# One wait per turn in place of many: two one-element reads of the last exponential in an attention kernel, and a tanh moved between two exponentials

## The chip, the cores and the metric

The kernel runs on one core of a Trainium2 chip. A core has five engines with a queue of instructions each: TensorE (matrix products; the profile's PE, its weight loads PEld), VectorE (DVE), ScalarE (ACT), GpSimd (POOL) and SyncE (SP, which here only starts DMA transfers). An engine takes its instructions in order. Between engines, and where one instruction must see what an earlier one of the same engine has written, order is kept by semaphores that an instruction waits on. The metric is the device time of one execution in microseconds (us).

## The reference

For a sequence of 2048 rows of width 512, with 32 heads of 16 and a hidden width of 1792:

```python
xn = layernorm(x)
q, k, v = split(xn @ wqkv)                        # 32 heads of width 16
s  = softmax(q @ k.T * 16**-0.5) @ v @ wo         # attention
h  = relu(xn @ w1 + b1) ** 2                      # dense layer, squared relu
g  = silu(h @ w2 + b2)
out = x + s * g
```

## The kernel before

The first part of the kernel normalizes x and forms the keys, queries and values. The main part is a loop of 128 **turns**. A turn handles four steps; a step is a block of 128 keys against 512 queries for four heads, in two pairs of heads. For each pair the scores come from two matmuls of 64 rows each, which lie in the two halves of TensorE's array and run at the same time (`score`, line 282). ScalarE takes their exponential into a tile `ptile` in SBUF (`exps`, line 286). At the end of the turn `values` (line 561) multiplies the four steps' exponentials with the values and adds up in PSUM, in 32 matmuls of a quarter of the array each.

PSUM has two score tiles S that take turns, one bank called `single` (its tile is named lin), one bank pair called `spare`, and the accumulator `acc`. In a turn the scores come in this order: the two pairs of step 1 and the two of step 2 go through S; the two pairs of step 3 are **set aside**: each half-pair goes to `single`, VectorE copies it to SBUF (`aside`, line 305, four copies a turn), and ScalarE later takes the exponential in place (`exps(i + 3, p, ptile[...])`); then come the two pairs of the next turn's first step, through S. So the last exponential of a turn is that of the next turn's step 0, second pair. A score tile is used again when its exponential has been taken. The second score of a turn, `scores(i + 1, 1)`, uses the tile of that last exponential.

The matmuls of the dense layer and of the last projection fill in between. A `Block` is a sum of such matmuls in one bank of `spare`; `lin`, `lin_part` and `swap` (lines 330 and 350) issue them half an array at a time, a schedule written out by hand in the turn loop. Per chunk of 512 rows the list `fill` has 28 entries, one for each turn: `make` starts a pair of blocks, `end` tells whether one finishes, a third flag whether a piece of the weights is split in two at the turn's end (`split_piece`, a cast on VectorE and a subtraction on GpSimd). When a pair is complete its `evict` runs on VectorE: bias, relu, square and a cast for the first layer (lines 413, 414, 100), one addition into `y` for the second (line 429).

Other work has due times: `at(time, fn)` puts it in a table, and `happen(n)` and `happen(n + 0.5)` issue what is due at the start of turn n and near its end. Among these are row sums (lines 583 to 595), loads, and the gate of the dense layer: `gate_start` (line 606, a tanh on ScalarE) and half a turn later `gate_end` (line 612, on VectorE, then a DMA). There are eight gates. After every fourth turn (n % 4 == 3) `finish` evicts the accumulator to `ou`, on VectorE, except in 12 turns where `turn_ends_first` sends that copy to ScalarE.

The loop runs under a manual schedule: each engine's queue has the order in which the code issues. The waits are worked out from the tiles that an instruction reads and writes. A tile `ptile` was last written by an exponential of the turn before, so an exponential that writes it again waits for ScalarE's own semaphore beside that of the scores, and the first of two set-aside copies into it waits for ScalarE beside TensorE. Where an instruction has two waits, the first is an instruction of its own ahead of it (EVENT_SEMAPHORE in the trace).

Of the kernel before, what the change touches and what calls it, by code (L numbers as in the profile page):

```python
# [24 lines left out]
FT = mybir.dt.float32  # L25
# [3 lines left out]
OP = mybir.AluOpType  # L29
# [44 lines left out]
def fast_path(tc, sb, ps, env):  # L74
# [7 lines left out]
    dve, act, pool, sp = nc.vector, nc.scalar, nc.gpsimd, nc.sync  # L82
# [3 lines left out]
    def t(shape, dt, tag):  # L86

        cnt[0] += 1
        p = ps if tag in ("S", "lin", "acc") else sb
        if tag in BUFS:  # L90
            turn[tag] = turn.get(tag, -1) + 1
            n = turn[tag] % BUFS[tag]
            tag = f"{tag}{places[n] if tag == 'S' else n}"
        return p.tile(shape, dt, tag=tag, name=f"{tag}_{cnt[0]}")
# [181 lines left out]
    ptile = {}  # L276

    def score(i, p, hp, dst):
        qd, qc, kb = steps[i]
        k, q = ka[qd, kb // 8], qa[qd, qc]  # L280
        r = slice(64 * hp, 64 * hp + 64)
        mm(dst, k[r, p, 128 * (kb % 8):128 * (kb % 8) + 128], q[r, p], start=True, stop=True)  # L282

    def exps(i, p, src):
        if src is not None:
            act.activation(ptile[i, p], src, AF.Exp, scale=SCALE)  # L286

    def place(i, p):
        ptile[i, p] = t([128, 2, 512], FT, f"P{2 * ((i - 1) % 4) + p}")

    def scores(i, p):

        if i < len(steps):
            sc = t([128, 2, 512], FT, "S")
            place(i, p)
            for hp in range(2):
                score(i, p, hp, sc[:, hp])
            return sc

    def aside(i, p, hp):  # L300

        if hp == 0:
            place(i, p)
        score(i, p, hp, single)
        dve.tensor_copy(ptile[i, p][:, hp], single)  # L305
# [51 lines left out]
    def lin(*halves):  # L357
        if pair[0]:
            for half in halves:
                j = half ^ swapped[0]  # L360
                pair[0][j].issue(half, lin_banks[j])

    def lin_part(half, part):
        if pair[0]:
            j = half ^ swapped[0]
            pair[0][j].issue_part(half, lin_banks[j], part)

    def swap():
        if pair[0]:
            while any([pair[0][half ^ swapped[0]].issue(half, lin_banks[half ^ swapped[0]]) for half in range(2)]):  # L370
                pass
            swapped[0] ^= 1
            if not swapped[0]:
                pair[0][0].evict()
                pair[0] = None
# [21 lines left out]
    def split_piece(eng=None):  # L397
        if at_piece[1] == len(pieces):
            return
        j, layer, m = pieces[at_piece[1]]  # L400
        at_piece[1] += 1
        raw, q = raws.pop(0), PAIRS[m][1]
        wf[layer, m] = [t([128, 4, 256] if layer == 1 else [128, 2, 512], FR, f"wf{layer}{p}{q}") for p in "hl"]
        split(*wf[layer, m], raw, eng or dve, pool)
        load_piece()
# [15 lines left out]
    def second(c, g, i):  # L421
        ms = [m for m in range(len(PAIRS)) if PAIRS[m][0] == g]
        h, w = [hid[m] for m in ms], [wf[2, m] for m in ms]

        def evict():
            if g == 0:
                y[c, i] = t([128, 2, 512], FT, f"y{i}")
            old = b2b.unsqueeze(1).broadcast_to([128, 2, 512]) if g == 0 else y[c, i]
            dve.tensor_tensor(y[c, i], spare, old, op=OP.add)
            if g == 3:  # L430
                complete.add((c, i))

        return [Block(lambda p, k, j=j: h[k // 2][p][:, k % 2, 128 * j:128 * j + 128],
                      lambda p, k: w[k // 2][p][:, k % 2], range(2 * len(ms)), evict)
                for j in (2 * i, 2 * i + 1)]
# [7 lines left out]
    fill = []  # L443
    for c in ORDER:
        for m, (g, _) in enumerate(PAIRS):
            fill += [(lambda m=m: first(m), False), (None, True)]
            if m in (1, 2, 4, 6):
                for i in range(2):
                    make = lambda c=c, g=g if m > 1 else 0, i=i: second(c, g, i)
                    fill += [(make, True)] if m == 1 else [(make, False), (None, True)]  # L450
    per = len(fill) // NC
    fill = [(*a, n % per in (0, 2, 4, 5, 6, 8, 10, 12, 14, 16, 18, 20, 22, 24)) for n, a in enumerate(fill)]
# [96 lines left out]
    def at(time, fn, *a):  # L549

        events.setdefault(int(2 * time), []).append((fn, a))
# [3 lines left out]
    def values(i):  # L555
        qd, qc, kb = steps[i]
        if kb == 0:
            acc[0] = t([128, 512], FT, "acc")
        for j in (1, 2, 3, 0) if i % 2 else (0, 1, 2, 3):
            o = (4 * qd + j) * 17  # L560
            mm(acc[0][32 * j:32 * j + 32], vt[:, kb, o:o + 32], ptile[i, j // 2][:, j % 2],  # L561
               start=kb == 0, stop=kb == NK - 1)

    def finish(i):

        qd, qc, kb = steps[i]
        if kb < NK - 1:
            return
        if i == len(steps) - 1:
            return  # L570
        ou = t([128, 512], FT, "ou")
        cast(act if turn_ends_first[0] else dve, ou, acc[0])
        sp.dma_start(zdram[qd][qc], ou[16::32])
        for j in range(4):
            sp.dma_start(udram[qd // 2][qc][0, qd % 2, :, j], ou[32 * j:32 * j + 16])
        n = i // 4
        events.setdefault(2 * n + 2, []).insert(0, (load_sums, (qd, qc)))
        at(n + 2, rowsums, qd, qc)
# [24 lines left out]
    def gate_start(c, i):  # L603
        assert (c, i) in complete
        e = t([128, 2, 512], FT, "T")
        act.activation(e, y[c, i], AF.Tanh, scale=0.5)
        gated[c, i] = e
# [98 lines left out]
        wlast.append(a)  # L706


    TURNS, LAST = len(steps) // 4, 16 * (NQ - 1)
    for n in range(4 * NQ - 1):  # L710
        at(4 * n + 0.5, load_qa, (n + 1) // 4, (n + 1) % 4)
# [4 lines left out]
        at(8.5 + 2 * kb + 2 * (kb > 9), maxvalue, kb)  # L716
    for j, c in enumerate(ORDER):
        for i in range(2):
            at(per * (j + 1) + 2 * i - 2, gate_start, c, i)
            at(per * (j + 1) + 2 * i - 1.5, gate_end, c, i)  # L720
        if j < 3:
            at(per * (j + 1) - 3.5, load_x_parts, ORDER[j + 1])
# [25 lines left out]
    fill = [(*a, 0) if len(a) == 2 else a for a in fill]  # L748
# [4 lines left out]
    def happen(time):  # L753
        for fn, a in events.pop(int(2 * time), ()):
            fn(*a)


    n = turn["S"]
# [4 lines left out]
    single = t([128, 512], FT, "lin")  # L763
    xs[0] = xT[3]

    def rest(i, dst):

        group(dst, lambda p: onorm[2, 3][p][:, cut[i]], lambda p: wos[0][p][:, 3])

    def end_rest(i, src):  # L770

        o = t([128, 512], FT, f"wf2{'hl'[i // 2]}{i % 2}")
        dve.scalar_tensor_tensor(o, src, 0.5, gsb[2, i // 2][:, i % 2], op0=OP.mult, op1=OP.mult)
        pool.dma_start(out[1024 + 128 * i:1152 + 128 * i], o, accum_op=OP.add)

    turn_ends_first = [False]
    for n in range(TURNS):
        i = 4 * n
        happen(n)
        make, end, split_now = fill[n]  # L780
        if make:
            pair[0] = make()
        exps(i + 1, 0, scores(i + 1, 0))
        aside(i + 3, 0, 0)
        lin(1)
        exps(i + 1, 1, scores(i + 1, 1))
        for _ in range(3):
            lin(0, 1)
        lin(0)
        if make and end:  # L790
            lin(1)
            lin(0)
            aside(i + 3, 0, 1)
        else:

            lin_part(1, 0)
            aside(i + 3, 0, 1)
            lin(0)
        exps(i + 2, 0, scores(i + 2, 0))
        if make and end:  # L800
            for j in range(2):
                pair[0][j].issue_whole(lin_banks[j])
            swap()
        else:
            lin_part(1, 1)
            lin(0, 1)
            lin(0, 1)
        exps(i + 2, 1, scores(i + 2, 1))
        aside(i + 3, 1, 0)
        lin(1)  # L810
        exps(i + 3, 0, ptile[i + 3, 0])
        lin(0, 1)
        lin(0, 1)
        last = [scores(i + 4, 0)]
        lin(0, 1)
        lin(0, 1)
        lin(0)
        aside(i + 3, 1, 1)
        exps(i + 3, 1, ptile[i + 3, 1])
        last.append(scores(i + 4, 1))  # L820
        for p in range(2):
            exps(i + 4, p, last[p])
        if n == TURNS - 1:
            two = t([128, 2, 512], FT, "S")
            rest(0, two[:, 0])
        turn_ends_first[0] = n < LAST and end and fill[n][0] is None and fill[n - 1][2] and n % per in (7, 15, 23)
        swap()
        if n == LAST - 1:
            gsb.update({(2, i): y[2, i] for i in range(2)})
        if n == TURNS - 1:  # L830
            end_rest(0, two[:, 0])
        happen(n + 0.5)
        if split_now:
            split_piece()
        for j in range(4):
            values(i + j)
        finish(i + 3)
# [169 lines left out]
```

## Time and profile before

| | us |
|---|---|
| median of 3 runs | 1262.85 (1262.16 to 1263.13) |
| profiled execution | 1262.52 |
| its span, first to last instruction | 1260.7 |
| TensorE matmul busy | 1247.7 |
| ScalarE busy | 1034.2 |
| VectorE busy | 677.8 |
| GpSimd busy | 259.0 |

The granted clock of TensorE is 0.998 of full speed over the whole span. The 128 turns run from 149.56 to the last values at about 1242. Most turns are 8.5 us long. A row of a timeline has the start in us from the span's start, the length, the engine, the line of the code, the operation, output and input tiles, the shapes and a count; in brackets stands how long the engine was idle before and what ended it. Matmuls are pipelined and overlap, so that the length of one is more than the time between two; the ends are modelled. A row of the waits has who waited for whom, the sum, how often, and the longest. Rows of groups have the busy time and, after the comma, the mean length of one in ns.

### The profile page before, as it was taken

To read this page: it belongs to the slowest core of one execution; us is meant where nothing else is said; L and a number is where in the kernel's file an instruction comes from. 1 tells how busy PE (TensorE), PEld (TensorE's weight loads), DVE (VectorE), ACT (ScalarE), POOL (GpSimd) and SP (SyncE) were. 2 spreads that over 40 slices of the span, in tenths; PEclk is the share of its full clock that TensorE was granted. 3 is DMA by queue.
4 is the path that set the end of the run, shared out by engine and by line. 5 is a ranking of instruction groups with operands and counts; after the bars stand their busy time and mean duration, and the time that the engine had idled before them with its cause. 6 is when DMAs were issued, how large, how long until landed. Compare 5 with 4: busy or idle time off the path is not lost.

```text
span 1260.7 us, 24997 instructions
## 1 busy us (share of the span) xinstructions
PE 1247.7 (99%) x10029; PEld 721.5 (57%) x10029; DVE 677.8 (54%) x1064; ACT 1034.2 (82%) x1123; POOL 259.0 (21%) x150
## 2 busy tenths in 40 slices
PE   9999999999999999999999999999999999999997
PEld 7888755555555555555555555555555555555553
DVE  5542255555555654545465455555554545566655
ACT  4222588989899898999988989899889989998883
POOL 5000122122211221312023221220331212322112
PEclk9999999999999999999999999999999999999999
DMA  7565613231233232131423222333222122463444
GB/s 267 209 234 190 218 49 105 60 94 52 85 127 110 60 97 72 42 92 46 154 75 110 59 78 60 93 126 106 59 62 90 46 90 59 144 218 125 145 131 119
DMA packets 84940, 137.32 MB, mean 109 GB/s; under 512 B 26058, under 2 KB 40408, under 8 KB 83284
## 3 DMA queue, kind: packets, MB, share of 16 engines
q1 hardware_dynamic: 81668, 126.25, 30.9%
q0 software_dynamic: 2720, 8.65, 2.4%
q8 instruction: 79, 1.29, 0.4%
q10 hardware_dynamic: 432, 0.79, 0.2%
q14 instruction: 41, 0.34, 0.1%
HBM read 94.24 MB, written 41.41 MB: 108 GB/s over the span
## 4 chain that ended last, share of the span: by engine, by line
PE 97%; DVE 1%; POOL 1%; issue 0%; DMA 0%; ACT 0%; DVEq 0%; ACTq 0%
PE acc L561 36%; PE spare L330 25%; PE S L282 16%; PE S L111 9%; PE lin L282 8%; PE spare L350 1%; PE S L204 1%; PE spare L339 0%; POOL hl L104 0%; DMA P<-in_A_x_dram 0%; PE acc L111 0%; DVE P L305 0%; DVE st L166 0%; POOL wf2l L104 0%; PE spare L687 0%
## 5 line engine op out<-in xcount | busy, mean ns | idle before, releaser
L286 ACT ACTIVATE P<-S 128x1024 f32<-128x1024 f32 x768 | 732.5, 1020 | 67.6 <-PE S L282 64.5
L305 DVE COPY P<-lin 128x512 f32<-128x512 f32 x512 | 353.8, 691 | 457.5 <-PE lin L282 412.7
L561 PE MATMUL acc<-P,vt 128*32 128x512 f32 x4096 | 466.0, 595 | 0.0
L282 PE MATMUL S<-QA,KA 64*128 64x512 f32 x1536 | 335.1, 417 | 0.1
L286 ACT ACTIVATE P<-P 128x1024 f32<-128x1024 f32 x256 | 271.3, 1060 | 34.4 <-DVE P L305 34.3
L561 PEld LDWEIGHTS acc<-P,vt 128*32 128x32 f32 x4096 | 120.0, 109 | 266.4 <-issue 266.4
L282 PEld LDWEIGHTS S<-QA,KA 64*128 64x128 f32 x1536 | 147.6, 184 | 160.6 <-ACT P L286 121.6
L282 PE MATMUL lin<-QA,KA 64*128 64x512 f32 x512 | 213.7, 417 | 0.7 <-DVE P L305 0.5
L104 POOL TENSOR_TENSOR wf1l<-wr,wf1h 128x1024 fp32r<-128x1024 f32 x28 | 66.8, 2384 | 400.8 <-DVE wf1h L100 137.9
L104 POOL TENSOR_TENSOR hl<-T,hh 128x1024 fp32r<-128x1024 f32 x28 | 67.7, 2417 | 240.3 <-DVE hh L100 129.6
L330 PE MATMUL spare<-xl,wf1h 64*128 64x512 f32 x440 | 109.6, 392 | 0.0
L282 PEld LDWEIGHTS lin<-QA,KA 64*128 64x128 f32 x512 | 94.1, 184 | 26.6 <-DVE P L305 4.0
L104 POOL TENSOR_TENSOR wf2l<-wr,wf2h 128x1024 fp32r<-128x1024 f32 x28 | 66.7, 2383 | 204.2 <-PE acc L561 138.0
L330 PE MATMUL spare<-wf2l,hh 64*128 64x512 f32 x400 | 97.4, 391 | 0.0
L330 PE MATMUL spare<-xh,wf1l 64*128 64x512 f32 x504 | 96.0, 391 | 0.0
L330 PE MATMUL spare<-xh,wf1h 64*128 64x512 f32 x504 | 95.6, 390 | 0.0
L330 PE MATMUL spare<-wf2h,hh 64*128 64x512 f32 x448 | 85.7, 390 | 0.0
L330 PE MATMUL spare<-wf2h,hl 64*128 64x512 f32 x416 | 80.8, 391 | 0.0
L330 PEld LDWEIGHTS spare<-xh,wf1h 64*128 64x128 f32 x504 | 59.9, 184 | 9.5
L98 ACT CAST P<-S 128x512 fp32r<-128x512 f32 x30 | 17.6, 587 | 57.6 <-PE S L111 55.8
L330 PEld LDWEIGHTS spare<-xh,wf1l 64*128 64x128 f32 x504 | 60.4, 185 | 7.6
L330 PEld LDWEIGHTS spare<-xl,wf1h 64*128 64x128 f32 x440 | 63.0, 184 | 1.5
(210 smaller groups left out, 1108.0 us busy)
## 6 DMA issues: line engine op xcount, KB each, us to landing
wr<-in_B_w_dram SPq DMA_DIRECT2D x56, 512.0 KB
KA<-kd SPq DMA_DIRECT2D x64, 256.0 KB
QA<-qd SPq DMA_DIRECT2D x128, 128.0 KB
kd<-P SPq DMA_DIRECT2D x15, 512.0 KB
qd<-P SPq DMA_DIRECT2D x15, 512.0 KB
u<-ud SPq DMA_DIRECT2D x15, 512.0 KB
P<-in_A_x_dram SPq DMA_DIRECT2D x8, 512.0 KB
xd<-KA SPq DMA_DIRECT2D x4, 1024.0 KB
```

What stands on the lines that cost most here:

```text
L98: act.copy(dst, src)
L104: leng.tensor_tensor(lo, src, hi.bitcast(FT), op=OP.subtract)
L111: mm(dst, lhs(a, k), rhs(b, k), start=n == 0, stop=n == len(todo) - 1)
L204: nc.tensor.transpose(pt[:, k, 128 * j:128 * j + 128], xnorm[c, i][:, j, 128 * k:128 * k + 128], ident)
L282: mm(dst, k[r, p, 128 * (kb % 8):128 * (kb % 8) + 128], q[r, p], start=True, stop=True)
L286: act.activation(ptile[i, p], src, AF.Exp, scale=SCALE)
L305: dve.tensor_copy(ptile[i, p][:, hp], single)
L330: mm(bank, self.lhs(a, k)[r], self.rhs(b, k)[r], start=n == 0 and self.at[other] == 0, stop=n == len(self.todo[half]) - 1 and self.at[othe ...
L350: mm(bank[:, c], self.lhs(a, k)[r], self.rhs(b, k)[r, c], start=False, stop=False)
L561: mm(acc[0][32 * j:32 * j + 32], vt[:, kb, o:o + 32], ptile[i, j // 2][:, j % 2], start=kb == 0, stop=kb == NK - 1)
```

## The change

A helper `see` is called in each turn but the first, after the turn's first score matmuls and ahead of its first exponential. On ScalarE it copies the last element of the tile that the last exponential of the turn before wrote. On VectorE it takes the maximum of that element and one element of the score tile that this exponential read. Each of the two waits for that last exponential; instructions behind it on the same engine then don't wait for ScalarE's semaphore, where they did for an earlier exponential. A further copy on VectorE of one element of `single` stands after the turn's last set-aside copy. The conditions in `alone` leave out some turns: both engines in the eight turns with a tanh, ScalarE where it evicts the accumulator at the turn's end, VectorE where n % 4 == 3 and ScalarE does not evict.

Since VectorE now reads the score tile of the last exponential, the second score of a turn, which uses that tile again, waits for VectorE's maximum where there is one, in place of the exponential. The first set-aside score of a turn waits for the added copy of `single`.

The tanh of a gate is issued in the same turn as before, not at its start ahead of the first exponential but between the two set-aside exponentials.

```diff
+    tanh_in = {}
...
-            at(per * (j + 1) + 2 * i - 2, gate_start, c, i)
+            tanh_in[per * (j + 1) + 2 * i - 2] = c, i
...
+    seen = t([1, 16], FT, "seen")
+
+    def see(i, other, act_waits, dve_waits):
+
+        last = ptile[i, 1][:1, 1, 511:]
+        if act_waits:
+            act.copy(seen[:, :1], last)
+        if dve_waits:
+            dve.tensor_tensor(seen[:, 8:9], last, other[:1, 0, :1], op=OP.max)
+
     for n in range(TURNS):
         i = 4 * n
         happen(n)
         make, end, split_now = fill[n]
+        turn_ends_first[0] = n < LAST and end and not make and fill[n - 1][2] and n % per in (7, 15, 23)
+
+        alone = [n not in tanh_in and not turn_ends_first[0],
+                 n not in tanh_in and (n % 4 < 3 or turn_ends_first[0])]
         if make:
             pair[0] = make()
-        exps(i + 1, 0, scores(i + 1, 0))
+        pair0 = scores(i + 1, 0)
+        if n:
+            see(i, last[1], *alone)
+        exps(i + 1, 0, pair0)
         aside(i + 3, 0, 0)
...
         exps(i + 3, 0, ptile[i + 3, 0])
+        if n in tanh_in:
+            gate_start(*tanh_in[n])
         lin(0, 1)
...
         aside(i + 3, 1, 1)
+        if alone[1]:
+            dve.tensor_copy(seen[:, 8:9], single[:1, :1])
         exps(i + 3, 1, ptile[i + 3, 1])
...
-        turn_ends_first[0] = n < LAST and end and fill[n][0] is None and fill[n - 1][2] and n % per in (7, 15, 23)
         swap()
```

In the changed kernel the copy on ScalarE is line 784, the maximum on VectorE line 786 and the copy of `single` line 840; the lines named above keep their numbers up to 707.

## The prediction

> **What bounds the kernel now.** I read the page first, for the share of each engine and the chain that ended last, then the waits, then the timeline of single turns, engine by engine.
>
> ```profile
> PE 1247.7 (99%) x10029; PEld 721.5 (57%) x10029; DVE 677.8 (54%) x1064; ACT 1034.2 (82%) x1123; POOL 259.0 (21%) x150
> ...
> PE 97%; DVE 1%; POOL 1%; issue 0%; DMA 0%; ACT 0%; DVEq 0%; ACTq 0%
> ```
>
> TensorE carries 97% of the chain. ScalarE is busy 82% of the span and has room. So nothing on ScalarE or VectorE counts until it makes TensorE late, and TensorE's queue is in order: one weight load that waits holds everything behind it. The waits (us in total, times, longest) say where that can be:
>
> ```profile
> PEld S L282 <- ACT P L286: 121.6, 198, 0.8
> ACT P L286 <- PE S L282: 64.5, 107, 0.9
> ```
>
> ScalarE waits for the first score of a turn 107 times at 0.6 us each. The 121.6 us are mostly not lost: the load is fetched ahead while matmuls still run. To see what is lost I take one plain turn, turn 50 (starts 576.21). Columns: start, length, engine, line, operation. Weight loads:
>
> ```profile
> 576.55 0.19 PEld L282 LDWEIGHTS S<-QA,KA 64*128 64x128 f32 x2
> ...
> 579.07 0.18 PEld L282 LDWEIGHTS lin<-QA,KA 64*128 64x128 f32 x1
> ```
>
> Its matmuls:
>
> ```profile
> 576.55 0.39 PE L282 MATMUL lin<-QA,KA 64*128 64x512 f32 x1
> ...
> 576.79 0.39 PE L282 MATMUL S<-QA,KA 64*128 64x512 f32 x2
> 577.02 1.08 PE L330 MATMUL spare<-xh,wf1h 64*128 64x512 f32 x7
> ...
> 577.83 0.46 PE L282 MATMUL lin<-QA,KA 64*128 64x512 f32 x1
> ...
> 579.17 0.63 PE L330 MATMUL spare<-xl,wf1h 64*128 64x512 f32 x2
> ...
> 579.88 0.40 PE L282 MATMUL S<-QA,KA 64*128 64x512 f32 x2
> ```
>
> Its copies on VectorE and its exponentials on ScalarE:
>
> ```profile
> 575.85 0.69 DVE L100 CAST hh<-T 128x1024 fp32r<-128x1024 f32 x1
> 577.05 0.69 DVE L305 COPY P<-lin 128x512 f32<-128x512 f32 x1 [0.51 <-PE lin L282]
> 578.33 0.69 DVE L305 COPY P<-lin 128x512 f32<-128x512 f32 x1 [0.59 <-PE lin L282]
> ```
>
> ```profile
> 575.20 1.02 ACT L286 ACTIVATE P<-S 128x1024 f32<-128x1024 f32 x1
> 576.82 3.79 ACT L286 ACTIVATE P<-S 128x1024 f32<-128x1024 f32 x4 [0.60 <-PE S L282]
> 580.49 1.06 ACT L286 ACTIVATE P<-P 128x1024 f32<-128x1024 f32 x1
> 581.83 1.06 ACT L286 ACTIVATE P<-P 128x1024 f32<-128x1024 f32 x1 [0.28 <-DVE P L305]
> ```
>
> The two halves of the array work side by side. In the row of seven, each half has four starts, so a slot is (1.08 - 0.39) / 3 = 0.23 us. From the score at 576.79 to the score at 579.88 the code issues 26 half-array matmuls (the two half-column ones counted as one), 13 slots: 2.99 us, but 3.09 passed. So TensorE stalls about 0.09 us a turn. The last place is the load at 579.07: the copy of 578.33 ended at 579.02, the load starts 0.05 later and its neighbour's matmul 0.10 after that. Turn lengths, by the windows (busy time per engine):
>
> ```profile
> 252.56:261.06 8.50, 8.50 (x77) 4.67 (x74) 5.38 (x10) 7.62 (x8) 1.61 (x1) 1.00 0.29 81
> 576.21:584.70 8.49, 8.49 (x77) 4.66 (x73) 3.70 (x6) 7.61 (x9) 4.70 (x2) 1.00 0.00 0
> 610.15:618.85 8.70, 8.70 (x78) 4.58 (x74) 3.89 (x5) 8.44 (x10) 0.00 (x0) 1.00 0.24 94
> 1140.01:1148.77 8.76, 8.76 (x74) 4.66 (x71) 5.60 (x11) 7.70 (x8) 2.96 (x3) 1.00 0.49 156
> ```
>
> An unstalled plain turn would be 8.49 - 0.09 = 8.40.
>
> **The change, part by part: what is saved.** The first copy of a turn waits for two semaphores (line 305 against TensorE and ScalarE), the second for one. The first starts 577.05 - (576.55 + 0.39) = 0.11 after its matmul, the second 578.33 - (577.83 + 0.46) = 0.04. A second wait costs 0.07 us when the engine stands ready. Where `see` waits once, the turn's first copy and first exponential start 0.07 earlier, and the loads that stall follow: I take 0.07 of the 0.09 (bounds 0 and 0.09). A rule of the Trainium skill speaks against the gain: VectorE: DVE Perf Modes, Rules for kernel authors, says to minimize the number of operations, not of semaphores. The 0.11 and 0.04 disagree with it; it is a rival below.
>
> **What is added.** One element each: 107 copies on ScalarE (L784), 99 maxima (L786) and 100 copies (L840) on VectorE, counted over the 128 turns from the conditions in `alone`. No DMA is added or moved, and SP's and POOL's queues keep their order. Nearest rows for a small operation:
>
> ```profile
> L518 ACT ACTIVATE warm<-eps 128x1 f32<-128x1 f32 x1 | 0.2, 203 | 0.0
> ...
> L856 DVE COPY zc<-lin 128x16 f32<-128x16 f32 x1 | 0.2, 175 | 0.1
> ```
>
> ScalarE's copy waits for the last exponential to finish (576.22) and lasts some 0.20: done by 576.47, inside the idle 0.60 before 576.82. It costs nothing there; its cover is gone if it lasts over 0.5, and then every 0.1 more is a 0.1 later exponential. VectorE's maximum also reads the bank of the last score, so the **second score of the turn now waits for VectorE** in place of ScalarE, in all 99 turns. That is the main cost. In TensorE's queue stand behind this load all other matmuls of the turn. The maximum waits for the last exponential, and for everything ahead of it in VectorE's own queue; I give it 0.17 (bounds 0, if only its start counts, and 0.20, the ScalarE row). With VectorE free: 576.22 + 0.04 + 0.17 + 0.05 = 576.48, before the load of 576.55. Such a load could be 0.13 later still without loss (0.23 of a slot less the 0.10 from load to matmul). So a maximum that ends later than 0.42 into the turn stalls TensorE by the excess. VectorE is late at the start of many turns; turn 12, and the evictions of the accumulator by engine:
>
> ```profile
> 249.49 1.21 DVE L429 TENSOR_TENSOR y<-spare,y 128x1024 f32<-128x1024 f32 x1
> 252.70 0.69 DVE L100 COPY ou<-acc 128x512 f32<-128x512 f32 x1 [1.99 <-PE acc L561]
> 253.40 0.69 DVE L305 COPY P<-lin 128x512 f32<-128x512 f32 x1
> ```
>
> ```profile
> L100 DVE COPY ou<-acc 128x512 f32<-128x512 f32 x19 | 13.1, 687 | 22.9 <-PE acc L561 22.9
> ...
> L98 ACT COPY ou<-acc 128x512 f32<-128x512 f32 x12 | 7.0, 588 | 1.8 <-PE acc L561 0.6
> ```
>
> In turn 12 (starts 252.56) VectorE evicts the accumulator from 252.70 to 253.39, when TensorE has finished it, and the maximum is queued behind. An operation can start about 0.08 before the end of the one ahead (turn 116 below: the copy at 1141.14, the eviction's end at 1141.22). So the maximum runs from 0.75 into the turn, and the score's matmul starts at 0.75 + 0.17 + 0.05 + 0.10 = 1.07 to 1.09, not at 0.58. TensorE loses 0.51; with the old 0.09 gone the turn grows by 0.42. Of the 19 evictions on VectorE 15 stand ahead of a turn with a maximum: eight are like turn 12, **+3.4 us**; four come behind a cast, three in the tail:
>
> ```profile
> 184.27 0.68 DVE L100 COPY ou<-acc 128x512 f32<-128x512 f32 x1
> ...
> 1140.55 0.67 DVE L100 COPY ou<-acc 128x512 f32<-128x512 f32 x1
> 1141.14 0.67 DVE L305 COPY P<-lin 128x512 f32<-128x512 f32 x1
> ```
>
> Turn 4 starts 183.97 and its eviction ends 0.98 in: stall 0.65, less 0.09, four times 0.55: **+2.2**. Turn 116 starts 1140.01 and its eviction ends 1.21 in: stall 0.88, against 0.36 now (8.76 - 8.40, since its first copy starts late, at 1141.14), three times 0.51: **+1.5**.
>
> The other turns. The 12 that follow an eviction on ScalarE: its copy ends late, and ScalarE's one-element copy now stands between it and the first exponential.
>
> ```profile
> 218.71 0.59 ACT L98 COPY ou<-acc 128x512 f32<-128x512 f32 x1 [0.15 <-PE acc L561]
> 219.19 1.03 ACT L286 ACTIVATE P<-S 128x1024 f32<-128x1024 f32 x1
> ```
>
> Turn 8 starts 218.57, its first exponential 0.62 in. At 0.72 to 0.82 the turn is 0.09 to 0.19 longer, by the tanh turn below (0.85 gives 8.70): eleven times 0.14, **+1.5**; the twelfth, turn 108, also has a late cast, +0.6. Next, even turns behind a cast:
>
> ```profile
> 269.26 0.69 DVE L100 CAST hh<-T 128x1024 fp32r<-128x1024 f32 x1
> ```
>
> ```profile
> 1157.29 0.62 DVE L100 CAST wf1h<-T 128x512 fp32r<-128x512 f32 x1
> ```
>
> In eight (turn 50: cast done 576.54, 0.33 in) the copy of L840 in the turn before pushes the cast by 0.1: stall 0.08, which the saved 0.09 pays. In five (turn 14 starts 269.55, cast done 0.40 in) the stall is 0.16: +0.4. Three in the tail (turn 118 starts 1157.23, cast done 0.68 in): +0.4, +0.4, +0.1. In 40 turns VectorE is early: 0.07 saved each, **-2.8**. Twelve have VectorE's second wait gone and not ScalarE's: -0.03 each, -0.4. Sixteen have no maximum: their copies keep both waits, nothing.
>
> **Tanh.** It moves from ahead of the first exponential to between the set-aside ones.
>
> ```profile
> 610.05 1.06 ACT L606 ACTIVATE T<-y 128x1024 f32<-128x1024 f32 x1
> 611.00 1.02 ACT L286 ACTIVATE P<-S 128x1024 f32<-128x1024 f32 x1
> ```
>
> ```profile
> 251.59 1.04 PE L561 MATMUL acc<-P,vt 128*32 128x512 f32 x8
> ```
>
> Now it delays the first exponential to 0.85 in, and the turn is 8.70. In its new place it fills the gap of 0.28 before 581.83 and pushes the last exponential 0.6 past the next turn's start. That turn starts its exponentials at 0.85 to 0.9 (the one-element copy waits for 0.61 + 0.04 and lasts 0.2), and its second score waits as long. Eight pairs: 8.70 + 8.49 = 17.19 before, 8.49 + 8.80 after, **+0.8**. The last eight value matmuls need that set-aside exponential; they start 0.97 before the next turn (251.59 against 252.56), so at 583.73 in turn 50, and the exponential would end at 581.83 + 0.6 + 1.06 = 583.49: no stall.
>
> **Sum.** 3.4 + 2.2 + 1.5 + 1.5 + 0.6 + 0.4 + 0.9 + 0.8 - 2.8 - 0.4 = +8.1 us. The profiled execution took 1262.52 around a span of 1260.7, 0.33 below the median of 1262.85: 1262.5 + 8.1 = 1270.6.
>
> **Rivals.**
> - *Faster.* The second score is not held, because the maximum is through before 0.42 into the turn everywhere. Then the 71 turns counted above with a maximum and no eviction on ScalarE each gain 0.07: -5.0 - 0.4 + 1.5 + 0.8 = -3.1, 1259.4. It decides where that maximum ends before 0.42. For it: VectorE is busy only 54%. Against: the eviction of turn 12 ends 0.83 in and cannot end sooner, it waits for TensorE.
> - *No change.* Second scores stall half as much (the maximum counts only with its start, part is caught up): of some 12 us of stall 6 go, +2, 1264.5.
> - *The saved waits are worth nothing.* That would keep only the losses, 8.1 + 2.8 + 0.4 = +11.3: 1273.8. Against: 0.11 and 0.04 after the matmul, above. By the Trainium skill's rule above this is the outcome.
> - *ScalarE's copy is not covered.* It lasts over 0.5, since it waits for its own engine's exponential; each 0.1 beyond is 0.1 in some 95 turns, so 0.2 beyond gives 1270.6 + 19 = 1290. Against: 0.20 in the row.
>
> **How the numbers follow.** My sum 0.53, worthless waits 0.13, uncovered copy 0.09, no change 0.12, faster 0.13. A measurement of this kernel tells about 0.2%, 2.5 us, from no change. Slower is 0.53 + 0.13 + 0.09 = 0.75. The range, 1259 to 1278, takes in half of the faster case, the middle, the worthless waits and stalls up to 1.6 times mine; it leaves out the uncovered copy. The forecast's own range is 1265.5 to 1276.
>
> **What would show it.** Turn 12's second pair of weight loads (L282) waits for VectorE's maximum and starts about 1.0 into the turn, not 0.34; that turn is 8.9 long. Plain turns with VectorE early are 8.42. The first copies start 0.04 after their matmul. ScalarE's copy ends before 0.5 into a plain turn. In the waits a new row stands, weight loads of S held by VectorE, 8 to 12 us lost. I am wrong if turn 12 stays at 8.5, or if plain turns gain more than 0.09.

## The result, and the profile after

The changed kernel takes 1267.24 us (median of 7 runs, 1266.61 to 1267.74), the kernel before 1262.46 beside it (7 runs, 1262.16 to 1263.19). The ratio is 1.0036, 95% interval 1.0025 to 1.0048: **slower by 0.36%, 4.8 us**. The profiled execution has a span of 1265.4 where before had 1260.7.

The page after, busy time by engine and the chain that ended last:

```profile
PE 1246.9 (99%) x10029; PEld 715.3 (57%) x10029; DVE 693.3 (55%) x1263; ACT 1056.0 (83%) x1230; POOL 258.9 (20%) x150
...
PE 91%; DVE 4%; issue 2%; ACT 1%; POOL 1%; DMA 0%; DVEq 0%; ACTq 0%
```

The busy time of TensorE has not grown; its share of the chain fell from 97% to 91%, and VectorE's rose from 1% to 4%. The waits (us in total, times, longest) say where VectorE came in:

```profile
PEld S L282 <- ACT P L286: 123.3, 218, 0.8
...
ACT P L286 <- PE S L282: 54.4, 131, 0.7
...
PEld S L282 <- DVE seen L786: 20.3, 46, 1.1
```

The last row is new: 46 weight loads of scores are held by the maximum of line 786. It counts the whole wait of a load, also the part that TensorE, still busy with matmuls, does not feel; how much of it is lost, e1 below shows. The three added instructions, by the groups of the page (busy, mean ns of one):

```profile
L784 ACT COPY seen<-P 1x1 f32<-1x1 f32 x107 | 20.3, 190 | 3.0
...
L786 DVE TENSOR_TENSOR seen<-P,S 1x1 f32<-1x1 f32 x99 | 13.7, 138 | 79.9 <-ACT P L286 79.9
L840 DVE COPY seen<-lin 1x1 f32<-1x1 f32 x100 | 13.6, 136 | 0.0
```

Now single turns, by the windows (start and end of the turn, then its length). They are, in this order, turn 4 (behind a cast and an eviction on VectorE), 8 (behind an eviction on ScalarE), 9 (plain), 12 (behind an eviction on VectorE), 54 (with a tanh), 55 and 57 (each after a tanh, 57 with a maximum) and 116 (tail):

```profile
184.10:193.51 9.41, 9.06 (x74) 4.39 (x71) 6.21 (x14) 8.10 (x10) 3.44 (x2) 1.00 0.25 71
219.32:227.87 8.55, 8.55 (x77) 4.57 (x74) 5.11 (x13) 8.15 (x11) 3.96 (x2) 1.00 0.28 79
227.87:236.29 8.42, 8.42 (x77) 4.60 (x73) 4.09 (x8) 7.82 (x10) 0.83 (x1) 1.00 0.30 80
253.20:262.09 8.89, 8.69 (x77) 4.55 (x73) 5.43 (x13) 7.91 (x10) 1.56 (x1) 1.00 0.29 77
612.20:620.69 8.49, 8.49 (x78) 4.78 (x74) 3.99 (x5) 7.89 (x9) 0.00 (x0) 1.00 0.14 55
620.69:629.26 8.57, 8.57 (x77) 4.60 (x74) 3.90 (x5) 8.29 (x10) 0.00 (x0) 1.00 0.16 60
637.75:646.51 8.76, 8.69 (x77) 4.57 (x74) 6.20 (x11) 8.40 (x11) 2.19 (x1) 1.00 0.46 135
1143.24:1152.51 9.27, 8.67 (x76) 4.58 (x72) 5.75 (x14) 7.97 (x10) 2.96 (x3) 1.00 0.58 174
```

Turn 12 went from 8.50 to 8.89 and turn 116 from 8.76 to 9.27; the plain turn lies at 8.42. Turn 4 was 8.82 before. Why turn 12 is longer: its weight loads after, and the rows before that answer to the last two,

```profile
253.20 0.19 PEld L282 LDWEIGHTS S<-QA,KA 64*128 64x128 f32 x2 [0.84 <-ACT P L286]
...
254.14 0.19 PEld L282 LDWEIGHTS S<-QA,KA 64*128 64x128 f32 x2 [0.64 <-DVE seen L786]
254.25 0.42 PEld L330 LDWEIGHTS spare<-xh,wf1h 64*128 64x128 f32 x4
```

```profile
252.90 0.19 PEld L282 LDWEIGHTS S<-QA,KA 64*128 64x128 f32 x2
253.13 0.65 PEld L330 LDWEIGHTS spare<-xh,wf1h 64*128 64x128 f32 x6
```

and VectorE's rows after:

```profile
253.35 0.69 DVE L100 COPY ou<-acc 128x512 f32<-128x512 f32 x1 [2.01 <-PE acc L561]
253.96 0.13 DVE L786 TENSOR_TENSOR seen<-P,S 1x1 f32<-1x1 f32 x1
```

The eviction holds VectorE until 254.04, the one-element maximum runs from 253.96, 0.76 into the turn, and the load of the second score waits for its end: 0.94 into the turn in place of 0.34. That load used to be fetched 0.13 ahead of need, so what follows it is late by less than 0.60: it starts at 1.05 (254.25) in place of 0.57 (253.13), 0.47 to 0.48 later. Further on 0.09 of that is caught up, and the turn ends 0.39 longer.

All 128 turns, after less before, in the classes of the prediction (a turn's length runs from the first score load to that of the next turn; mean of the class in us, then its sum):

| turns | each | sum | predicted sum |
|---|---|---|---|
| 8 like turn 12 | +0.41 | +3.27 | +3.4 |
| 4 behind a cast too (4, 32, 60, 88) | +0.57 | +2.28 | +2.2 |
| 3 tail evictions (116, 120, 124) | +0.49 | +1.48 | +1.5 |
| 11 behind an eviction on ScalarE | +0.05 | +0.58 | +1.5 |
| turn 108 | +0.57 | +0.57 | +0.6 |
| 13 even turns behind a cast | -0.03 | -0.39 | +0.4 |
| 3 tail casts (118, 122, 126) | +0.23 | +0.69 | +0.9 |
| 8 tanh turns and the 8 behind them | -0.20, +0.15 | -0.37 | +0.8 |
| 40 early turns | -0.07 | -2.89 | -2.8 |
| 12 with VectorE's wait alone gone | -0.01 | -0.15 | -0.4 |
| 16 without a maximum | -0.01 | -0.22 | 0 |
| start of the turns, turn 0 | | +0.15 | 0 |
| sum | | +5.0 | +8.1 |

### The profile page after: what moved, and what is told of

Its sections match the earlier page's. It is cut to its first block, busy times and chain, and to the rows that moved or that the text cites. A ratio compares the mean times of both kernels' runs of the same rounds, so it can differ in the third digit from the quotient of the medians.

```text
span 1265.4 us, 24423 instructions
## 1 busy us (share of the span) xinstructions
PE 1246.9 (99%) x10029; PEld 715.3 (57%) x10029; DVE 693.3 (55%) x1263; ACT 1056.0 (83%) x1230; POOL 258.9 (20%) x150
## 4 chain that ended last, share of the span: by engine, by line
PE 91%; DVE 4%; issue 2%; ACT 1%; POOL 1%; DMA 0%; DVEq 0%; ACTq 0%
PE acc L561 32%; PE spare L330 25%; PE S L282 16%; PE S L111 9%; PE lin L282 6%; ACT P L286 1%; PE spare L350 1%; DVE T L413 1%; DVE P L305 1%; PE S L204 1%; DVE T L414 0%; DVE T L677 0%; PE spare L339 0%; POOL hl L104 0%; DVE ou L100 0%
## 5 line engine op out<-in xcount | busy, mean ns | idle before, releaser
L282 PE MATMUL S<-QA,KA 64*128 64x512 f32 x1536 | 340.0, 418 | 5.5 <-DVE seen L786 5.1
L282 PEld LDWEIGHTS S<-QA,KA 64*128 64x128 f32 x1536 | 152.7, 183 | 181.7 <-ACT P L286 123.3
L282 PE MATMUL lin<-QA,KA 64*128 64x512 f32 x512 | 206.1, 402 | 0.7 <-DVE P L305 0.5
L330 PE MATMUL spare<-xl,wf1h 64*128 64x512 f32 x440 | 105.5, 391 | 0.0
L330 PEld LDWEIGHTS spare<-xl,wf1h 64*128 64x128 f32 x440 | 60.0, 184 | 1.3
```

Of the source, the lines that this page charges most:

```text
L330: mm(bank, self.lhs(a, k)[r], self.rhs(b, k)[r], start=n == 0 and self.at[other] == 0, stop=n == len(self.todo[half]) - 1 and self.at[othe ...
```

## The experiments

The theory was that the maximum's read of the score bank costs the time, since TensorE then waits for VectorE, late in some turns, and that the saved waits gain 0.07 in each early turn. The main rival was that the added instructions cost by themselves, or the move of the tanh.

**e1: VectorE no longer reads the score bank.** It still waits for the last exponential, by copying the element that this wrote.

```diff
-            dve.tensor_tensor(seen[:, 8:9], last, other[:1, 0, :1], op=OP.max)
+            dve.tensor_copy(seen[:, 8:9], last)
```

> The changed kernel, but VectorE's one element is copied from the last exponential's tile alone and the score tile is not read, so the second score waits for ScalarE again; every saved wait stays saved. Theory 'held score' (the second score waits for VectorE's queue): turn 12 falls from 8.89 to about 8.47, turn 4 from 9.41 to about 8.87, turn 116 from 9.27 to about 8.83, the 40 early turns stay at 8.42, the turns after a tanh at about 8.57: 1257.5 us, 5 below the kernel before. Rival 'worthless waits and extra operations' (the cost lies in the 306 added operations themselves): turn 12 stays near 8.9 and the time near 1267.

Measured: 1257.31 us (1256.72 to 1258.29), ratio to the kernel before 0.9959 (0.9945 to 0.9973). Turn 12 of this kernel, which starts at 252.38, VectorE's rows and then the load of its second score:

```profile
252.53 0.69 DVE L100 COPY ou<-acc 128x512 f32<-128x512 f32 x1 [1.99 <-PE acc L561]
253.14 0.13 DVE L786 COPY seen<-P 1x1 f32<-1x1 f32 x1
```

```profile
252.73 0.19 PEld L282 LDWEIGHTS S<-QA,KA 64*128 64x128 f32 x2
```

The small instruction stands at the same place (0.76 into the turn), just as late; but nobody waits for it, and the second load is back at 0.35. Turns 4 and 12 by the windows:

```profile
183.78:192.66 8.88, 8.88 (x74) 4.61 (x70) 6.26 (x14) 8.02 (x10) 3.46 (x2) 1.00 0.30 78
252.38:260.82 8.44, 8.44 (x77) 4.65 (x73) 5.42 (x13) 7.81 (x10) 1.55 (x1) 1.00 0.30 80
```

They are 8.88 and 8.44 where the change has 9.41 and 8.89. The instruction is a copy here and a maximum there, but it lasts 0.13 in both; what differs is the operand in the score bank. That operand costs 1267.24 - 1257.31 = 9.9 us (the prediction had 8 to 12 us lost in this wait), and it alone turns a gain into a loss. By class, e1 less the change: the 8 like turn 12 -3.7, the four -2.2, the three -1.3, the tail casts -0.9, behind a tanh -0.8, casts -0.7, turn 108 -0.5.

**e2: no small instructions on VectorE in the 15 turns behind an eviction there**, all else as in the change.

```diff
...
+        if n and n % 4 == 0 and not evicted_by_act:
+            alone[1] = False
+        evicted_by_act = turn_ends_first[0]
```

> The changed kernel, but without VectorE's maximum (and the copy of single) in the turns that follow an eviction on VectorE (15 turns: 4, 12, 20, 32, ... 124); the rest as changed. Theory 'held score': these 15 turns carry 3.3 + 2.3 + 1.5 = 7.0 us, so they return to 8.49, 8.82 and 8.7 and the time to about 1260.2. Rival 'spread cost' (the loss lies in all turns with a maximum): 15 of 99 turns give back about 1 us, 1266.

Measured: 1261.10 us (1259.79 to 1261.82), ratio 0.9990 (0.9981 to 0.9999). Turns 4 and 12:

```profile
183.90:192.70 8.80, 8.80 (x74) 4.57 (x70) 6.10 (x12) 7.91 (x10) 3.48 (x2) 1.00 0.30 78
252.39:260.88 8.49, 8.49 (x77) 4.74 (x73) 5.40 (x11) 7.82 (x10) 1.60 (x1) 1.00 0.30 80
```

They are as long as before the change (8.82 and 8.50). Those 15 turns, 3.27 + 2.28 + 1.48 = 7.0 us by the table, carried the loss; 6.1 us of it came back in the median. (Two other turns of the profiled execution, 39 and 115, are 0.3 longer; the last section has them.)

**e3: the kernel before with only the tanh moved.**

```diff
...
-            at(per * (j + 1) + 2 * i - 2, gate_start, c, i)
+            tanh_in[per * (j + 1) + 2 * i - 2] = c, i
...
         exps(i + 3, 0, ptile[i + 3, 0])
+        if n in tanh_in:
+            gate_start(*tanh_in[n])
```

> The kernel before with the tanh moved alone, no one-element operations. By my prediction's step for tanh (+0.8 us in the changed kernel, with the one-element operations in the turn behind): here the turn of the tanh falls from 8.69 to 8.49 and the next grows by about 0.1 (second score waits for the exponential that ends 0.6 in): -1.6 + 0.8 = -0.8, 1261.7 us. Rival: the late exponential delays the values too, each pair costs 0.2: 1264.

Measured: 1261.74 us (1261.04 to 1262.54), ratio 0.9995 (0.9986 to 1.0004), which is no difference that this can tell. Turns 54, 55 and 57:

```profile
609.73:618.22 8.49, 8.49 (x77) 4.77 (x73) 3.99 (x5) 7.89 (x10) 0.00 (x0) 1.00 0.17 66
618.22:626.83 8.61, 8.61 (x77) 4.56 (x74) 3.89 (x5) 8.27 (x9) 0.00 (x0) 1.00 0.16 61
635.31:643.95 8.64, 8.64 (x77) 4.57 (x73) 6.06 (x9) 8.30 (x9) 2.21 (x1) 1.00 0.44 137
```

The tanh's own turn falls from 8.70 to 8.49, and the next one rises from 8.49 by 0.12 to 0.15. Over the eight pairs the two sums are -1.30 and +0.77 (turns 82 and 113 among them had been long before for another reason, and turn 82 is so here; the last section has both). The tanh is not part of the loss.

**e4: ScalarE's copy alone** (the changed kernel without lines 786 and 840).

```diff
-            see(i, last[1], *alone)
+            see(i, last[1], alone[0], False)
...
-        if alone[1]:
-            dve.tensor_copy(seen[:, 8:9], single[:1, :1])
```

> The changed kernel without VectorE's two one-element operations: ScalarE's copy and the moved tanh stay. Theory: in a plain turn the loads that stall last wait for VectorE's copies, so ScalarE's earlier exponential alone gains at most 0.02 a turn, the 12 turns behind an eviction on ScalarE lose 0.1 each; with the tanh -0.8: about 1261.8 us, plain turns 8.48. Rival: ScalarE's first exponential sets the stall, plain turns fall to 8.42 and the time to 1257.

Measured: 1262.05 us (1261.33 to 1262.48), ratio 0.9997 (0.9988 to 1.0006). Turn 9 starts at 227.19; its rows on ScalarE and on VectorE:

```profile
227.15 0.19 ACT L784 COPY seen<-P 1x1 f32<-1x1 f32 x1
227.73 1.94 ACT L286 ACTIVATE P<-S 128x1024 f32<-128x1024 f32 x2 [0.39 <-PE S L282]
```

```profile
228.03 0.69 DVE L305 COPY P<-lin 128x512 f32<-128x512 f32 x1 [1.89 <-PE lin L282]
```

The first exponential starts 0.54 in, as in the change, in place of 0.60; the first set-aside copy still at 0.84. The turn is 8.49 long and has gained nothing: the median of the 40 early turns is -0.003.

**e5: VectorE's two instructions alone.**

```diff
-            see(i, last[1], *alone)
+            see(i, last[1], False, alone[1])
```

> The changed kernel without ScalarE's one-element copy: VectorE's two stay, with the score tile read, and the moved tanh. Theory: the held scores stay (3.3 + 2.3 + 1.5 us in the 15 turns behind an eviction on VectorE, 0.6 and 0.7 in turn 108 and three of the tail), and the early turns lose most of their gain, because the exponentials stall next: 8.47 instead of 8.42, as in the 12 turns that lack ScalarE's saved wait. The 11 turns behind an eviction on ScalarE give back 0.6. In all 1269 us. Rival: ScalarE's copy itself delays the turns, so that taking it away gains: 1265 or less.

Measured: 1270.43 us (1269.80 to 1270.73), ratio 1.0064 (1.0050 to 1.0077). Turns 9 and 12:

```profile
227.60:236.08 8.48, 8.48 (x77) 4.62 (x73) 4.09 (x7) 7.64 (x9) 0.83 (x1) 1.00 0.27 79
253.05:262.00 8.95, 8.74 (x77) 4.55 (x73) 5.40 (x12) 7.73 (x8) 1.56 (x1) 1.00 0.27 77
```

All of the loss is here, and 1.4 us more than the 1269 expected: the held turns are somewhat longer than in the change (turn 12 at 8.95 for 8.89). There is little of the gain: the early turns have a median of -0.019, although their first copy starts 0.77 in. With e4 this says that the first exponential and the first copy both have to start earlier. Each alone gains 0.003 and 0.019 a turn, both together 0.067.

**e6: the changed kernel without the copy of line 840.** The first set-aside copy then has two waits again, for TensorE and for VectorE.

```diff
-        if alone[1]:
-            dve.tensor_copy(seen[:, 8:9], single[:1, :1])
```

> The changed kernel without the copy of one element of single. In 50 turns, the early ones among them, the first set-aside copy then waits for VectorE itself beside TensorE, two waits as before the change; casts at a turn's end come 0.1 earlier. If the saved second wait of the first copy is what an early turn gains, these turns go back from 8.42 to about 8.49: +2.9 us, less 0.5 for the casts, 1269.6 us. If the gain has another source, the early turns stay at 8.42 and the time falls a little below 1267.

Measured: 1266.73 us (1266.36 to 1266.96), ratio 1.0035 (1.0021 to 1.0048). This missed: I had expected the early turns to lose their gain. They keep it (median -0.065). Turn 9, VectorE and then its length:

```profile
227.60 0.14 DVE L786 TENSOR_TENSOR seen<-P,S 1x1 f32<-1x1 f32 x1 [1.02 <-ACT P L286]
228.39 0.69 DVE L305 COPY P<-lin 128x512 f32<-128x512 f32 x1 [0.65 <-PE lin L282]
```

```profile
227.63:236.07 8.44, 8.44 (x77) 4.69 (x74) 4.03 (x7) 7.79 (x10) 0.75 (x1) 1.00 0.25 80
```

The copy starts 0.76 in, with two waits. The trace's records of the wait instructions tell the difference (turn 9; times into the turn):

| kernel | wait instruction, starts | it waits for | the copy itself waits for | copy starts |
|---|---|---|---|---|
| before | 0.77 | TensorE, late | ScalarE, met long before | 0.84 |
| after | none | | TensorE, late | 0.78 |
| e6 | -0.02 | VectorE, met at once | TensorE, late | 0.76 |

So a second wait as such costs nothing here. What cost 0.07 is that the wait which is met last stood in the separate instruction, and the copy started 0.064 after that one. (The semaphores differ too, ScalarE's before and VectorE's in e6; no run swaps the two waits and nothing else.)

**e7: the loss taken out, the gain in more turns.** As e1; besides, no small instruction on VectorE behind an eviction there but one also where n % 4 == 3; ScalarE's copy is left out in the turn behind its eviction and no longer in the turn that ends with one.

```diff
...
-        alone = [n not in tanh_in and not turn_ends_first[0],
-                 n not in tanh_in and (n % 4 < 3 or turn_ends_first[0])]
+        alone = [n not in tanh_in and not evicted_by_act,
+                 n not in tanh_in and (n % 4 > 0 or evicted_by_act)]
+        evicted_by_act = turn_ends_first[0]
```

> What the runs point to: VectorE copies its element from the exponential's tile alone (no score tile read, as in the first run), not in turns behind an eviction on VectorE, but also where n % 4 == 3; ScalarE's copy is left out in the turn behind an eviction on ScalarE and not in the turn that ends with one; the tanh as changed. Theory: 80 turns or so at 8.42 (-5.2), tanh pairs -1.2, nothing lost elsewhere: about 1255.5 us, 7 below the kernel before. Rival: another stall comes next and keeps it at the 1257.3 of the first run.

Measured: 1254.85 us (1254.54 to 1255.22), ratio 0.9940 (0.9926 to 0.9953), faster than both kernels. Turns 8, 11 and 12:

```profile
218.21:226.71 8.50, 8.50 (x77) 4.71 (x74) 5.19 (x12) 8.10 (x9) 3.97 (x2) 1.00 0.29 79
243.58:252.00 8.42, 8.42 (x78) 4.60 (x75) 4.06 (x7) 7.82 (x10) 0.75 (x1) 1.00 0.22 64
252.00:260.48 8.48, 8.48 (x79) 4.75 (x75) 5.41 (x11) 7.80 (x10) 1.61 (x1) 1.00 0.29 81
```

Turn 11, one of the 16 that had no maximum, now gains too (median -0.06 over the 16), turn 8 is back at 8.50, and turn 12 keeps its old length.

## Why the prediction was right, and where it was off

**Direction and main cause: right.** The second score waits for VectorE, in the turns that were named. e1 takes that wait away, with the instruction still in its place, and the loss is gone; e2 takes the instructions out of the 15 turns, and 6.1 of their 7.0 us go. The three largest terms came out at 3.27, 2.28 and 1.48 for 3.4, 2.2 and 1.5. For turn 12 the single steps hold: maximum at 0.76 (0.75 forecast), rest of the queue late by 0.47 (0.51), and 0.09 of that paid by the old stall. The maximum lasts 0.13 there, not the 0.17 that I gave it.

**The saved waits: the size nearly right, the reason not quite.** The 40 early turns gave -2.89 for -2.8, with 8.42 for the plain turn as forecast, and the first copy 0.04 after its matmul. That the sums agree is partly luck: two of the turns (90 and 121) had been long before for another reason, told below, and give -0.62 of it; the other 38 gain 0.06 each for 0.07. And the step "a second wait costs 0.07 us when the engine stands ready" fails in e6: it is the late one of two waits, standing in an instruction of its own, that costs. The rival here, worthless waits at 1273.8, did not come, since turns did gain. Behind it stood the rule of the Trainium skill (VectorE: DVE Perf Modes, Rules for kernel authors), to minimize operations and not semaphores; e6 agrees with the rule as far as it goes: the copy with a second semaphore, met early, starts no later (0.76). Last, I put a gain of 0.03 on the 12 turns where VectorE's wait alone goes; they gain 0.01, as e5's early turns do (0.019).

**ScalarE's one-element copy and the turns behind a tanh: mis-sized.** These two terms make 2.1 of the 3.1 us between +8.1 and +5.0 (1.5 less 0.58, and 0.8 with -0.37). I let the copy delay the exponential behind it by up to the 0.20 of the nearest row. Turn 8 (starts 219.32) and turn 57 (starts 637.75) on ScalarE:

```profile
219.47 0.59 ACT L98 COPY ou<-acc 128x512 f32<-128x512 f32 x1 [0.25 <-PE acc L561]
219.95 0.18 ACT L784 COPY seen<-P 1x1 f32<-1x1 f32 x1
220.04 1.01 ACT L286 ACTIVATE P<-S 128x1024 f32<-128x1024 f32 x1
...
638.36 0.19 ACT L784 COPY seen<-P 1x1 f32<-1x1 f32 x1
638.45 1.92 ACT L286 ACTIVATE P<-S 128x1024 f32<-128x1024 f32 x2
```

The record is 0.18 to 0.19 long, as the row said, but the exponential starts 0.09 after the copy's start. So the first exponential of turn 8 is at 0.72, the low end of my 0.72 to 0.82, and the eleven turns cost 0.58 for +1.5. In turn 57 it is at 0.70 and not at 0.85 to 0.9; that turn is 8.76 long (8.80 forecast). Half of the turns behind a tanh (55 and its like, n % 4 == 3) have no maximum at all, which I overlooked: their second score waits only for the late exponential, and they are 8.57. The eight pairs gave -0.37 in place of +0.8. Most of that comes from the overlooked four (0.19 each below turn 57, 0.8 in all) and not from the copy's price; another 0.26 are long turns of the kernel before, told below.

**Casts: mis-sized by 0.8.** I had the saved wait used up in these turns. In the eight like turn 50 about half of it was kept (sum -0.25). In the five like turn 14 I expected +0.08 each, and four gave +0.02. The fifth, turn 98, is one of the long turns below and makes 0.2 of the 0.8. e6, where the cast comes 0.1 earlier, has turn 14 at 8.47 for 8.50.

**The rivals.** *Faster* needed a maximum that is through before 0.42 into every turn; it ended at 0.89 in turn 12. e1 shows how much that rival was worth: 1257.3, below its 1259.4. *No change* needed half of the stalls to be caught up; only the 0.09 was. *ScalarE's copy not covered*: it ends 0.18 into a plain turn, long before the first exponential at 0.54.

## What to carry to other kernels

Before an instruction on a busy engine reads a buffer that an in-order engine will refill, look at who is waited for next: the refill then waits for the last reader, and a one-element read behind a 0.69 us eviction cost 0.4 to 0.6 us a turn here. To spare a wait, read something that nobody is about to overwrite: e1 kept the gain that way. And cost a small instruction by the start of the next one on its engine, not by the length of its record.

## What the runs showed of the hardware beyond that

**Which of two waits stands alone.** The table of e6: of two waits, the one met last cost 0.06 to 0.07 us more when it stood in the separate instruction than when the working instruction carried it.

**Behind a separate wait an instruction at times starts 0.3 us late.** Turn 67 before the change (starts 721.50, 8.73 long), matmuls of the scores and then ScalarE:

```profile
721.50 0.50 PE L282 MATMUL S<-QA,KA 64*128 64x512 f32 x2
```

```profile
722.38 1.03 ACT L286 ACTIVATE P<-S 128x1024 f32<-128x1024 f32 x1 [0.89 <-PE lin L282]
```

The scores end at 722.00; by the records of the wait instructions the one ahead of this exponential ran at 722.04, and the exponential started 0.34 behind it, where 0.06 is usual. Turns 67, 90, 98 and 121 are 0.22 to 0.31 longer than in the change, which has 8.42 to 8.51 there. Turns 82 and 113 of the kernel before have such a start too (8.78 where the other tanh turns have 8.64 to 8.69, and 8.75 where 29, 57 and 85 have 8.49). In the table these six turns give the change about 1.2 us which no step of the prediction counted; without them its sum would be about +6.2, nearer to the +8.1.

Such starts stand in e3 (790.1 and 923.9 among them) and in e5 (794.2 and 928.9) too, which keep ScalarE's separate waits. The kernels with the copy of line 784 have 346 separate waits on ScalarE where the kernel before has 1102, and the change, e1, e2, e4 and e6 have one such start each, in turn 7 (214.24 in the change, 0.35 behind its wait, the turn 8.57 long for 8.49); e7 has none. VectorE has them as well: 0.42 to 0.43 behind a separate wait, twice in e2 (485.9 and 1133.0, which are its turns 39 and 115) and once each in e3 and e4 (850.1, 850.2).

Their place is not chance. Number the records of an engine's instructions in order, waits included, from 0: then each of these starts has a number that is 63 above a multiple of 128. On ScalarE before the change they are 1215, 1471, 1599, 1727, 1983 and 2111, in the change 191; on VectorE 575 and 1343 in e2, and 959 in e3 and e4. Kernels whose queue for the engine is the same have them in the same turns (67, 75 and 90 of ScalarE in e3 and e5, 82 of VectorE in e3 and e4), and an instruction more or less moves them: e2, without VectorE's small ones in 15 turns, has two there, the change none. Where such a number falls on an instruction whose engine is still busy, nothing is lost: number 319 in the change starts 0.10 before the exponential ahead of it ends, as others do. In the trace a packet of the instruction queue (q14 in the page, 41 packets before, of 8192 bytes in the turns) follows each of these starts by 0.6 to 3.8 us. A pause of the engine's sequencer around the fetch of instructions would fit, but the traces show the place and not the cause; no run was made for it, and it stays open.
